# One batch's loads moved to another DMA queue and later in the order, with its features re-dealt between two engines

## The chip, the cores and the metric

The kernel runs on one core of a Trainium2 chip. The metric is the device time of one execution in microseconds (us). The core has a matrix engine (TensorE, PE in the profile; its weight loads are listed as PEld), a vector engine (VectorE, DVE), a scalar engine (ScalarE, ACT), GpSimd (POOL) and SyncE (SP). SP does no arithmetic here: it only issues DMAs. A name with a q behind it (SPq, POOLq) is the instruction queue of that engine.

## The reference

Eight batches of cosine-weighted linear attention (8 heads, 576 positions, 64 dimensions) feed a two-layer network with a squared ReLU between its layers.

```python
def phi(x, c, s):
    r = np.maximum(x, 0.0)
    return np.concatenate([r * c, r * s], axis=-1)
q_p = phi(q, cos_w, sin_w)
k_p = phi(k, cos_w, sin_w)
kv = np.einsum('bhsf,bhsd->bhfd', k_p, v)
z = np.sum(k_p, axis=2)
num = np.einsum('bhsf,bhfd->bhsd', q_p, kv)
den = np.einsum('bhsf,bhf->bhs', q_p, z)[..., None] + 1e-06
x = (num / den)          # to [batch * position, head * dimension] = 4608 x 512
h = x @ w_in             # 512 -> 2048
g = np.maximum(h, 0.0) ** 2
out = g @ w_out          # 2048 -> 512
```

All inputs and the output are float32; the products run in bf16.

## The kernel before

**Attention of one batch.** The 576 positions are cut in four pieces of 128 (j = 0 to 3) and a tail of 64 (j = 4). For each batch b and piece j there are these steps, each a small function:

- `load_batch`, `load` (L61 to L77): three tensors from HBM, each as one DMA of 1 MB and two of 64 KB (the tails, `kt`, `vt`, `qt`). The input buffers are double, so batch 3 reuses batch 1's.
- `att_k` (L190): the features of k, a cosine half and a sine half, `kp`. The sine half is always made by ACT (`feat_sin`, L181), the cosine half by DVE (`feat_cos`, L171) or ACT (`feat_cos_act`, L186).
- `att_v` (L194): a copy of v to bf16, `vext`, by DVE or ACT (L200).
- `att_kv` (L222): the products of k features and v on PE (`kz`, L241), in two parts, and a copy of the sum to `kvz` by ACT.
- `att_feat` (L254): the features of q, `qp`, cosine half by DVE, sine half by ACT.
- `att_qT` (L259): from batch 2 on, the transposition of `qp` by a DMA that SP issues (L267), two pieces at a time: `qpT<-qp` twice, `qpT<-qpt` for the tail.
- `att_d`: `att_num` on PE (`num`, L310) and `att_div` on DVE (L320 to L324), which writes `x`.
- `att_x` (L331): from batch 2 on, the transposition of `x` by a DMA that SP issues (L342): `xT<-x` twice, `xTt<-xt` for the tail.

**The two layers of the network.** They are cut in slots of about 1.75 us of PE work. `gemm1` (L361) is the first layer: 16 or 32 matmuls into a PSUM tile `hps` (L383), then a ReLU on ACT (`rt`, L391) and a square on DVE (`gT`, L398). The first half of a batch's slots reads the first `xT`, the second half the second. `gemm2` is the second layer. From batch 1's second pair on it is a seven-product scheme (`pair_mm`, L541): products `p1` to `p7` go through four PSUM tiles `ya`, `yc`, `yu`, `yv`, each used for one product after another. A tile is free again only when ACT has copied it (`s1`, L561, `s5`, L576) or DVE has added it on (L537). `hps`, `yu` and `yv` share two PSUM buffers in turn.

**The order.** Everything is in the order of the program text. There are 144 slots, numbered from 0. A table `after` tells what is emitted behind each slot, and it is filled by calls `at(slot, function, ...)`, mostly through `plan` (L625). Work registered for the same slot is emitted in the order of registration. The slots that matter here:

| slots | work on PE | start in the profile, us |
|---|---|---|
| 16 to 25 | batch 1, layer 1 | 53.75 |
| 26 to 33 | batch 1, layer 2 | 74.82 |
| 34 to 41 | batch 2, layer 1 (34 to 37 read the first `xT` of batch 2, 38 to 41 the second) | 91.56 |
| 42 to 49 | batch 2, layer 2 (two pairs) | 109.81 |
| 50 to 59 | batch 3, layer 1 | 123.62 |

Batch 3's attention runs beside slots 27 to 41, batch 4's beside slots 42 to 54, and so on. `first[b]` and `second[b]` are the numbers of a batch's first slots of layers 1 and 2 (`second[2]` is 42, `first[3]` is 50).

**The queues.** Batch 0's inputs are loaded by SP. The weights and the inputs of batches 1, 2 and 3 are loaded by POOL, batch 3's behind slot 14. From batch 4 on SP loads, with k and v at one slot and q at a later one. SP's list is therefore, in this order: batch 2's three query transposes, then transposes of `x` of batch 2 and of queries of batch 3 in turn, with the k and v loads of batch 4 among them. The results of batches 0 to 6 are written by POOL (`put`, L401), one DMA of 512 KB for two pieces. Each SP DMA also waits, before it is issued, until the DMA eight places earlier in that list has landed; eight semaphores are used in turn.

Of the kernel before, what the change touches and what calls it, by code (L numbers as in the profile page):

```python
# [19 lines left out]
def kernel(  # L20
# [9 lines left out]
    nc = tc.nc  # L30
# [13 lines left out]
    NS = J + 1  # L44
# [562 lines left out]
    slots, first, second = [], {}, {}  # L607
# [6 lines left out]
    def at(s, fn, *args):  # L614
        after.setdefault(s, []).append((fn, args))
# [6 lines left out]
        att_qT_pe(b, j)  # L622
        att_qT_copy(b, j)

    def plan(b, k, f, kv, d, t=(), x=(), shared=True):  # L625


        for j in range(NS):
            last = j == J or j % 2
            at(k[j], att_k, b, j, feat_cos_act if shared and j % 2 else feat_cos)  # L630
            at(k[j], att_v, b, j, nc.scalar if shared and (b > 2 or j % 2) else nc.vector)
            at(f[j], att_feat, b, j)
            if t:
                at(t[j], att_t, b, j)
            elif last:
                at(f[j], att_qT, b, j // 2)
            at(d[j], att_d, b, j)
            if x:
                at(x[j], att_x_pe, b, j, x[j] > 16)
            elif last:  # L640
                at(d[j], att_x, b, j // 2)
        for i in range(2):
            at(kv[i], att_kv, b, i)


    for j in (2, 3):
# [8 lines left out]
    at(18, att_d, 0, J)  # L655
    at(19, att_x_pe, 0, J, True)
    plan(
        1,
        k=(8, 8, 8, 9, 9),
        f=(4, 5, 6, 12, 13),  # L660
        kv=(10, 10),
        d=(11, 13, 15, 17, 19),
        t=(5, 6, 7, 16, 17),
        x=(12, 14, 16, 18, 20),
        shared=False,
    )
    at(14, load_batch, 3, nc.gpsimd, "qkv")
    plan(
        2,
        k=(21, 22, 23, 24, 25),  # L670
        f=(18, 19, 20, 22, 23),
        kv=(26, 26),
        d=(27, 28, 29, 31, 33),
    )
    plan(
        3,
        k=(30, 32, 33, 34, 35),
        f=(27, 29, 31, 32, 33),
        kv=(36, 36),
        d=(37, 38, 39, 40, 41),  # L680
    )
    for b in range(4, B):
        o, p = second[b - 2], first[b - 1]
        at(second[b - 3] + 6, load_batch, b, nc.sync, "kv")
        at(first[b - 2] + 9, load_batch, b, nc.sync, "q")
        plan(
            b,
            k=(o, o, o + 1, o + 1, o + 2),
            f=(o + 4, o + 4, o + 5, o + 5, o + 6),
            kv=(o + 3, o + 4),  # L690
            d=[p + j for j in range(NS)],
        )

# [95 lines left out]
```

## Time and profile before

| what | value |
|---|---|
| median of 4 runs | 294.12 us (293.37 to 296.67) |
| the profiled execution | 294.11 us |
| its span, first to last instruction | 292.2 us |
| PE busy | 281.7 us, 96% of the span |
| DVE, ACT, POOL busy | 201.7, 164.7, 39.0 us |
| moved by DMA | 53.04 MB, mean 181 GB/s |
| matrix clock granted | 1.00 |

In the profile a group of instructions is shown as `line engine op out<-in`. A timeline line gives the start in us from the start of the span, the duration in us, and the count (x16). Brackets at its end give the time that the engine stood idle just before, and what ended that idle time. A DMA issue is timed by its issuing instruction; the DMA view adds the time from issue to landing.

### The profile page before, as it was taken

The page shows a single profiled execution, that of the slowest core. Times are in us where ns is not written, and L with a number is a line of the kernel's source. Part 1 is how long each engine was busy: PE and PEld are TensorE (multiplying, and loading weights), DVE is VectorE, ACT ScalarE, POOL GpSimd, SP SyncE. Part 2 cuts the span into 40 slices and gives each one's busy share as a digit, 9 for nine tenths or more (in the row PEclk, how much of TensorE's full clock was granted, in tenths as well). Part 3 has the DMA queues.
Part 4 walks back from the last instruction along what each step waited for, and adds up shares of the span by engine and source line. Part 5 has one row for each costly group of instructions (what it writes and reads, how often), then busy time and mean ns, then how long its engine had stood idle before and what let it go on. Part 6 is the DMA issues. An engine that isn't in the chain of part 4 may idle for free.

```text
span 292.2 us, 7292 instructions
## 1 busy us (share of the span) xinstructions
PE 281.7 (96%) x3045; PEld 236.4 (81%) x3045; DVE 201.7 (69%) x450; ACT 164.7 (56%) x251; POOL 39.0 (13%) x67
## 2 busy tenths in 40 slices
PE   8999999998999979999999999999999999999994
PEld 3469855788668969898988888988998988889883
DVE  2367765596399497977688777977677877546584
ACT  3476653679748758645783258835595551165110
POOL 1462504850000000000002000000000000000011
PEclk9999999999999999999999999999999999999999
DMA  7999995999638996699619995299718520300014
GB/s 208 291 203 285 343 219 174 341 375 295 101 103 159 283 199 194 163 266 284 190 71 189 291 236 164 82 249 305 184 56 206 141 46 2 143 3 2 0 76 142
DMA packets 76641, 53.04 MB, mean 181 GB/s; under 512 B 52000, under 2 KB 71712, under 8 KB 76608
## 3 DMA queue, kind: packets, MB, share of 16 engines
q1 hardware_dynamic: 66816, 29.24, 43.2%
q0 software_dynamic: 9648, 23.20, 26.8%
q8 instruction: 24, 0.39, 0.5%
q10 hardware_dynamic: 144, 0.13, 0.1%
q14 instruction: 9, 0.07, 0.1%
HBM read 36.70 MB, written 9.44 MB: 158 GB/s over the span
## 4 chain that ended last, share of the span: by engine, by line
PE 75%; DMA 10%; DVE 5%; ACT 3%; issue 2%; SPq 2%; POOL 1%; DVEq 0%; POOLq 0%
PE hps L383 36%; PE ya L525 9%; PE yc L525 8%; PE yu L525 7%; DMA q<-in_q_dram 6%; PE yv L525 4%; PE num L310 3%; PE kz L241 3%; DMA out_dram<-ysb 2%; PE yps L456 2%; DMA qpT<-qpt 2%; DVE ysb L537 1%; ACT rt L391 1%; SPq L69 1%; PE yps L432 1%
## 5 line engine op out<-in xcount | busy, mean ns | idle before, releaser
L383 PEld LDWEIGHTS <-w1sb 128*128 128x128 bf16 x1312 | 112.9, 98 | 13.7 <-issue 2.9
L383 PE MATMUL hps<-xT,w1sb 128*128 128x256 bf16 (+1 forms) x1056 | 119.0, 269 | 1.1 <-DVE ysb L537 0.6
L391 ACT ACTIVATE rt<-hps 128x1024 bf16<-128x1024 f32 x72 | 73.7, 1024 | 66.7 <-PE hps L383 43.3
L398 DVE TENSOR_TENSOR gT<-rt 128x1024 bf16<-128x1024 bf16 x64 | 44.0, 687 | 21.3 <-ACT rt L391 21.3
L525 PEld LDWEIGHTS <-gs 128*128 128x128 bf16 x480 | 46.9, 98 | 5.5
L525 PEld LDWEIGHTS <-gT 128*128 128x128 bf16 x312 | 29.8, 98 | 3.5
L410 POOL DMA_DIRECT2D out_dram<-ysb x14 | 7.6, 543 | 173.7 <-DVE ysb L537 145.8
L181 ACT ACTIVATE kp<-k,sin_col 128x512 bf16<-128x512 f32 x32 | 22.4, 719 | 2.9 <-DMA k<-in_k_dram 2.9
L324 DVE TENSOR_TENSOR x<-num,rden 128x512 bf16<-128x512 f32 x32 | 22.1, 691 | 1.1
L181 ACT ACTIVATE qp<-q,sin_col 128x512 bf16<-128x512 f32 x32 | 22.1, 724 | 0.8 <-DMA q<-in_q_dram 0.8
L320 DVE TENSOR_SCALAR den<-num 128x8 f32<-128x8 f32 (+1 forms) x40 | 6.5, 164 | 21.4 <-PE num L310 21.4
L521 DVE TENSOR_TENSOR gs<-gT 128x1024 bf16<-128x1024 bf16 x26 | 17.8, 685 | 0.0
L171 DVE TENSOR_SCALAR qp<-q,cos_col 128x512 bf16<-128x512 f32 x32 | 14.9, 492 | 1.8 <-DMA q<-in_q_dram 1.8
L383 PE MATMUL hps<-xTt,w1sb 128*128 128x128 bf16 x256 | 15.1, 219 | 0.8 <-ACT rt L391 0.8
L525 PE MATMUL yc<-w2sb,gs 128*128 128x256 bf16 x120 | 15.6, 273 | 0.0
L525 PE MATMUL ya<-w2t,gs 128*128 128x256 bf16 x120 | 15.6, 273 | 0.0
L525 PE MATMUL yu<-w2sb,gs 128*128 128x256 bf16 x120 | 15.6, 273 | 0.0
L525 PE MATMUL yu<-w2t,gs 128*128 128x256 bf16 x120 | 15.5, 272 | 0.0
L200 ACT CAST vext<-v 128x512 bf16<-128x512 f32 x23 | 14.2, 617 | 2.1 <-DMA v<-in_v_dram 2.1
L576 ACT COPY s<-yu 128x256 f32<-128x256 f32 x15 | 5.6, 373 | 17.3 <-PE yu L525 17.3
L310 PEld LDWEIGHTS <-qpT 128*128 128x128 bf16 (+1 forms) x240 | 10.3, 100 | 4.0 <-DMA qpT<-qpt 1.8
L525 PE MATMUL yc<-w2sb,gT 128*128 128x256 bf16 x104 | 13.5, 273 | 0.0
(93 smaller groups left out, 337.3 us busy)
## 6 DMA issues: line engine op xcount, KB each, us to landing
out_dram<-ysb POOLq DMA_DIRECT2D x14, 512.0 KB, 4.3
k<-in_k_dram SPq DMA_DIRECT2D x5, 1024.0 KB, 8.3
v<-in_v_dram SPq DMA_DIRECT2D x5, 1024.0 KB, 9.3
q<-in_q_dram SPq DMA_DIRECT2D x5, 1024.0 KB, 5.4
q<-in_q_dram POOLq DMA_DIRECT2D x3, 1024.0 KB, 12.6
k<-in_k_dram POOLq DMA_DIRECT2D x3, 1024.0 KB, 9.5
v<-in_v_dram POOLq DMA_DIRECT2D x3, 1024.0 KB, 8.5
w1sb<-in_moe_w_in_dram POOLq DMA_DIRECT2D x4, 512.0 KB, 9.1
```

The source lines that it names most:

```text
L171: nc.vector.tensor_scalar(out=dst[:, :, 0:D], in0=src, scalar1=0.0, scalar2=cos_col[:, j : j + 1], op0=ALU.max, op1=ALU.mult,)
L181: nc.scalar.activation(out=dst[:, :, D:F], in_=src, func=ACTF.Relu, scale=sin_col[:, j : j + 1])
L200: copy(out=vx[:, j, h0:h1, 0:D], in_=piece("v", b, j)[:, h0:h1, :])
L241: nc.tensor.matmul(out=kz[:, half, hh * E1 : (hh + 1) * E1], lhsT=lhsT, rhs=rhs, start=(j == 0 and hh == 0), stop=(j == J and hh == HH - 1),)
L310: nc.tensor.matmul(out=out, lhsT=lhsT, rhs=kvz[:, half * HH + hh, :], start=True, stop=True)
L324: nc.vector.tensor_tensor(out=x_of(b, j).rearrange("p (b k) (l d) -> p b k l d", b=n, l=2), in0=n4[:, :, :, 0:D].rearrange("p b (k l) d -> ...
L383: nc.tensor.matmul(out=out, lhsT=w1sb[:, kb, hb * P : (hb + 1) * P], rhs=rhs, start=(kb == 0), stop=(kb == KB - 1),)
L391: nc.scalar.activation(out=rt[:, :, :], in_=hps[:, :, :], func=ACTF.Relu)
L398: nc.vector.tensor_tensor(out=dst, in0=rt[:, :, :], in1=rt[:, :, :], op=ALU.mult)
L410: eng.dma_start(out=dst, in_=y.rearrange("p i c -> p (i c)") if n > 1 else y[:, c0:c1])
L521: nc.vector.tensor_tensor(out=t[:, :, :], in0=in0, in1=in1, op=op)
L525: nc.tensor.matmul(out=acc, lhsT=lhs[:, hb, :], rhs=rhs[:, hb, :], start=(hb == 0), stop=(hb == HB2 - 1),)
```

## The change

Four things are changed in `plan` and in the calls of `at`:

1. `load_batch(3, ...)` is moved from POOL at slot 14 (order q, k, v) to SP at slot 23 (order k, v, q). There it stands behind batch 2's third query transpose.
2. For batch 2, the cosine halves of k pieces 1 and 3 go from ACT to DVE, and so does the copy of v piece 3.
3. For batch 3, all cosine halves of k but the tail's go to ACT; the k and v slots are one or two earlier, the q feature slots three to six later, `att_kv` one later, and the divisions (`att_d`, with the transposes of `x` that follow them) two later, at slots 39 to 43.
4. For batch 4, the k and v loads go from slot 32 to slot 30. For batches 4 to 7, the two parts of `att_kv` go one slot later.

```diff
-    def plan(b, k, f, kv, d, t=(), x=(), shared=True):
+    def plan(b, k, f, kv, d, t=(), x=(), act_cos=(1, 3), act_v=range(NS)):
...
-            at(k[j], att_k, b, j, feat_cos_act if shared and j % 2 else feat_cos)
-            at(k[j], att_v, b, j, nc.scalar if shared and (b > 2 or j % 2) else nc.vector)
+            at(k[j], att_k, b, j, feat_cos_act if j in act_cos else feat_cos)
+            at(k[j], att_v, b, j, nc.scalar if j in act_v else nc.vector)
...
-        shared=False,
+        act_cos=(),
+        act_v=(),
     )
-    at(14, load_batch, 3, nc.gpsimd, "qkv")
     plan(
         2,
         k=(21, 22, 23, 24, 25),
         f=(18, 19, 20, 22, 23),
         kv=(26, 26),
         d=(27, 28, 29, 31, 33),
+        act_cos=(),
+        act_v=(1,),
     )
+    at(23, load_batch, 3, nc.sync, "kvq")
     plan(
         3,
-        k=(30, 32, 33, 34, 35),
-        f=(27, 29, 31, 32, 33),
-        kv=(36, 36),
-        d=(37, 38, 39, 40, 41),
+        k=(29, 30, 31, 32, 33),
+        f=(33, 34, 35, 36, 36),
+        kv=(37, 37),
+        d=(39, 40, 41, 42, 43),
+        act_cos=(0, 1, 2, 3),
     )
     for b in range(4, B):
         o, p = second[b - 2], first[b - 1]
-        at(second[b - 3] + 6, load_batch, b, nc.sync, "kv")
+        at(30 if b == 4 else second[b - 3] + 6, load_batch, b, nc.sync, "kv")
         at(first[b - 2] + 9, load_batch, b, nc.sync, "q")
         plan(
             b,
             k=(o, o, o + 1, o + 1, o + 2),
             f=(o + 4, o + 4, o + 5, o + 5, o + 6),
-            kv=(o + 3, o + 4),
+            kv=(o + 4, o + 5),
             d=[p + j for j in range(NS)],
         )
```

In SP's list the order around the change becomes: three query transposes of batch 2; k, v, q of batch 3 (nine DMAs); the first `xT` of batch 2; k, v of batch 4 (six DMAs); the second `xT` and the `xTt` of batch 2; three query transposes of batch 3; two `xT` and the `xTt` of batch 3; q of batch 4.

## The prediction

> **What bounds the kernel now.** I read the page first, then PE's timeline for its idle time, then the DMA views and SP's timeline between 60 and 140 us.
>
> ```profile
> span 292.2 us, 7292 instructions
> PE 281.7 (96%) x3045; PEld 236.4 (81%) x3045; DVE 201.7 (69%) x450; ACT 164.7 (56%) x251; POOL 39.0 (13%) x67
> PE 75%; DMA 10%; DVE 5%; ACT 3%; issue 2%; SPq 2%; POOL 1%; DVEq 0%; POOLq 0%
> ```
>
> PE is the bound. Whatever the change gains must be PE's idle time, and its timeline shows where that lies in the changed stretch:
>
> ```profile
> 73.03 1.95 PE L383 MATMUL hps<-xTt,w1sb 128*128 128x128 bf16 x32 [0.84 <-ACT rt L391]
> 78.01 0.30 PE L241 MATMUL kz<-vextt,kpt 64*128 64x65 bf16 x8 [0.33 <-ACT kpt L181]
> 91.56 5.40 PE L383 MATMUL hps<-xT,w1sb 128*128 128x256 bf16 x48 [0.63 <-DVE ysb L537]
> 109.56 0.32 PE L310 MATMUL num<-kvz,qpT 128*64 128x65 bf16 x8 [1.52 <-DMA qpT<-qpt]
> ```
>
> Four waits, 0.84 + 0.33 + 0.63 + 1.52 = 3.3 us: the most that can be gained, 1.1% of the time. (About 1% is also what a measurement of this kernel can tell from no change.) From 110 us on PE hardly waits, so nothing later can be won back.
>
> ```profile
> 83.65 1.23 SPq L342 DMA_TRANSPOSE xT<-x  x1
> 94.34 1.71 SPq L64 DMA_DIRECT2D k<-in_k_dram  x1
> 110.78 1.48 SPq L342 DMA_TRANSPOSE xTt<-xt  x1
> 112.31 0.57 SPq L64 DMA_DIRECT2D q<-in_q_dram  x1
> 118.24 0.53 POOL L410 DMA_DIRECT2D out_dram<-ysb  x1 [24.57 <-DVE ysb L537]
> ```
>
> The first `xT` of batch 2 is issued at 83.65, before any load in SP's list. The DMA view, for windows around single issues, gives its time to landing (3.0 us at 83.65) and that of one issued at 133.90 behind batch 5's k and v (5.0 us):
>
> ```profile
> xT<-x SPq DMA_TRANSPOSE x1, 3.0
> xT<-x SPq DMA_TRANSPOSE x1, 5.0
> q<-in_q_dram SPq DMA_DIRECT2D x1, 1024.0 KB, 5.4
> qpT<-qp SPq DMA_TRANSPOSE x1, 9.2
> ```
>
> The reader is to see that a transpose lands after what stands before it in the list (it landed at 138.89, v's last tail at 138.07), and that the query transpose issued at 64.81 took 9.2 us while POOL's loads of batch 3 ran.
>
> **What the Trainium skill says.** "DMA: Bandwidth & Descriptors", section Queues, rings and completion order: on each DMA engine descriptors are consumed in ring order. The trace agrees: SP's DMAs land in their order of issue from 60 to 140 us. The same page, section Issuing engines are not separate DMA queues: DMAs of all issuers share the same 16 engines; the 9.2 us show it. "PSUM — Partial Sum Buffer", section Engine vs sequencer instructions: ScalarE and VectorE are strict FIFO, so a feature that waits for a load holds up the PSUM copies behind it. The trace agrees in that every ACT and DVE instruction starts in program order.
>
> **Part 1, slots 20 to 33: the gain.** ACT loses two cosine halves (0.61 us from start to start) and one copy of v (0.51), 1.73 us of the stretch from 69.6 to 77 in which it runs without a pause. DVE takes 0.40 + 0.40 + 0.34 = 1.1 us there, where it waits 1.58 and 1.23 us for ACT: free. `rt` of slot 23 then starts at 71.36 instead of 71.98, so slot 25 starts at 72.3 instead of 73.03, and the tail's k feature is done before PE asks. Gain 1.1 us by slot 27. DVE loses five or more features of batch 3 (0.39 each) before slot 34, so its 0.63 us should go as well. Slot 34 could start at 91.56 - 1.1 - 0.6 = 89.9.
>
> **Part 2, the loads in SP's list: the loss.** The third query transpose of batch 2 waits for ACT's tail feature (now 73.4) and lands about 77.3. Behind it come 3.54 MB. After a change from transposes to loads the first tensor landed 4.4, 5.3 and 5.1 us after the last transpose (batches 4, 5, 7); I take 5.0. The next tensors follow at 3.3 to 4.2 us (batches 0, 2, 4, 5, 7); I take 3.7. POOL's write of batch 1's first results, 0.5 MB at about 84, takes the engines 1.6 us: in the packets from 127 to 128 us the write moved 0.34 MB and SP's ring 0.015. So k lands at 82.3, v between 86 and 87.6, q at 77.3 + 5.0 + 3.7 + 3.7 + 1.6 = 91.3.
>
> ACT wants k at 83.5 (there) and v at 84.8: it waits 1 to 3 us, and `s1` behind it is copied at about 87 to 88 where `p6` wants its tile at 86.8. That stall of up to 1.5 us is not added, since the next is longer: the first `xT` of batch 2, ready to issue at 82.4, stands behind these loads and lands 0.9 after q (as for batch 5), at 92.2. **Slot 34 starts at 92.2, not at 89.9.** Then k and v of batch 4 (4.2 + 3.7) and POOL's next write (1.6) stand before the second `xT`: 92.2 + 9.5 + 0.9 = 102.6. PE wants it after four slots and batch 3's `kz`, 4 x 1.75 + 1.36 = 8.4, at 100.6. **Slot 38 starts at 102.6.** Slot 42 follows after 4 x 1.75 and three `num` (0.24 each), at 110.3. Before it was 109.81, with two `num` more behind it: 109.3 at equal work. Loss +1.0 us, with all four old waits already credited. Bounds: loads at 326 GB/s throughout (batch 0's second and third tensor) give slot 34 at 90.4, slot 38 at 99.7, slot 42 at 107.4, -1.9 us; all costs at their upper ends give +3.
>
> The query transposes of batch 3 come next at 2.2 us each (512 KB): 105.3, 107.5, 108.3. `num` asks at 106.1 at the earliest, so the old 1.52 us wait does go.
>
> **Part 3, q of batch 4.** Its load stays at slot 43 but stands behind `xTt` of batch 3, which waits for the fifth division. That moves from slot 41 to 43. Counted from slot 42's start: `x` done at 4.8, `xTt` issued until 6.3 (1.48), q at +5.4 = 11.7. Before: issued 2.5, landed 7.9 to 8.4, used at 8.4: no slack. Now POOL's write of batch 2's first results (issued at 8.6) falls into it: +1.5, so 13.2. The users stay at slot 46. DVE stands at `qp` before the addition that frees `yc`: 13.2 + 0.8 + 0.35 = 14.4, where `p7` wants it at 12.3. Stall 2.1, of which 0.1 is made good at slot 50. Then `qpT` of batch 4 is issued at 14.5 and lands 4.2 later at 18.7, where `num` wants it at 18.0: 0.65. Together +2.6 us; without the clash with the write 1.1.
>
> **Parts at nothing.** `att_kv` one slot later for batches 4 to 7: `kvz` is used three or more slots later; if that cover were gone it would cost one 0.5 us copy each. Batch 5's k and v about 3.5 us later: landed at 138.07, used after 142.7 plus the delay. POOL's queue without nine DMAs lets batch 0's results leave earlier; nobody waits for them. The later divisions of batch 3 are used at slot 50: free.
>
> Sum: 294.11 + 1.0 + 2.6 = **297.7 us**. The profiled execution is at the median of 294.12, so no shift.
>
> **Rivals.**
> A, forecast: both `xT` and q late, 297.7, own range 296.0 to 299.5; chance 0.50.
> B, fast loads: -1.9 + 2.6 gives 294.8. For it: batch 0's second and third tensor. Against: after transposes the first tensor needed 5 us three times. Chance 0.22.
> C, slow loads: every cost of part 2 at its upper end (+3) and q's clash with the write at 2.1 instead of 1.5 us (+3.2) gives 300.3. For it: three writes of 0.5 MB fall into the stretch, and batch 5's k took 6.2 us from its first packet under one. Against: it needs all of them at once. Chance 0.20.
> D, not slower: the transposes do not stand behind the loads. Place: the first `xT` at slot 34. If it lands before 89.9 and the second before 98, all 3.3 us are gained, and q's delay of 1.1 to 2.6 is paid: 292.7. It decides from that landing. For it: batch 5's transpose lost only 2 us behind loads, because it was issued late. Against: no SP DMA overtook another. Chance 0.08. That the features' move brings nothing (ACT was not what held slot 25) would change the sum only by hiding 1.7 us of gain behind waits that end later anyway.
>
> **How the numbers follow.** Three quarters of A and all of C lie above 297.05 (+1%): 0.57 slower. The rest of A, B and most of D: 0.40 same. Faster by 1% needs all 3.3 us without q's price: 0.03. The range leaves out D, the low end of B and the high end of C: 294.5 to 300.5.
>
> **What would show it.** Right: PE waits at slot 34 for `xT` (about 2 us), at slot 38 (2 us), at `yc` near slot 48 (2 us), and no wait at slot 25, nor for `qpt` at slot 41. ACT waits for v. The first `xT` takes more than 6 us to land. Wrong: `xT` landing within 3 to 4 us of its issue, or q of batch 3 before 88.

## The result and the profile after

Over the timed executions (44 of the changed kernel, 63 of the kernel before) the ratio is **1.0072, 95% interval 1.0056 to 1.0088**: slower by 0.7%, which is 2.1 us on the 293.52 us that the kernel before had in this set. Ratios, here and below, leave out executions more than 1.5% above the fastest of their kernel (here 6 of the 44 and 2 of the 63), while medians, here 296.31 and 293.52 us or 0.95% apart, count all of them. The profiled execution took 297.63 us, 3.5 us more than the profiled one of before (294.11). The changed kernel's executions scatter more than those of before, 293.68 to 300.35 us, and the profiled one lies in the slower half. Times and profile are therefore kept apart below.

The page after, in its three lines on the whole:

```profile
span 295.9 us, 7290 instructions
PE 283.1 (96%) x3045; PEld 236.4 (80%) x3045; DVE 202.1 (68%) x451; ACT 164.2 (56%) x250; POOL 32.6 (11%) x58
PE 71%; DMA 16%; DVE 6%; POOL 2%; issue 1%; ACT 1%; SPq 1%; DVEq 0%; ACTq 0%
```

DMA's share of the chain that ended last rose from 10% to 16%, but this tells little of the change: 33 of its 48 us are three loads before 41 us (`v` 8.6, `q` 14.1, `w2sb` 10.4), which the change does not touch. PE's timeline shows where the changed kernel waits (start, duration, what, and in brackets the idle time before it and what ended it):

```profile
72.53 1.95 PE L383 MATMUL hps<-xTt,w1sb 128*128 128x128 bf16 x32 [0.23 <-ACT rt L391]
92.69 8.83 PE L383 MATMUL hps<-xT,w1sb 128*128 128x256 bf16 x64 [2.65 <-DMA xT<-x]
102.65 3.67 PE L383 MATMUL hps<-xT,w1sb 128*128 128x256 bf16 x32
110.63 1.03 PE L525 MATMUL ya<-w2sb,gT 128*128 128x256 bf16 x8
124.98 1.03 PE L525 MATMUL yc<-w2sb,gs 128*128 128x256 bf16 x8 [1.39 <-DVE ysb L537]
127.09 1.91 PE L383 MATMUL hps<-xT,w1sb 128*128 128x256 bf16 x16 [0.20 <-DVE ysb L537]
```

The reader is to see three things. The wait of 0.84 us at slot 25 has shrunk to 0.23, and the waits at `kz`'s tail (0.33) and for `qpt` (1.52) are gone. Slot 34, at 92.69, now waits 2.65 us for the first `xT` of batch 2. And near 125 us PE waits 1.39 us for an addition on DVE. DVE came late to that addition because it had stood waiting for q of batch 4, and so had ACT, as their timelines show:

```profile
123.71 0.88 DVE L171 TENSOR_SCALAR qp<-q,cos_col 128x512 bf16<-128x512 f32 x2 [2.15 <-DMA q<-in_q_dram]
124.51 0.42 DVE L537 TENSOR_TENSOR ysb<-yc,s 128x256 f32<-128x256 f32 x1
123.71 1.33 ACT L181 ACTIVATE qp<-q,sin_col 128x512 bf16<-128x512 f32 x2 [4.47 <-DMA q<-in_q_dram]
```

The DMA view for windows around the first `xT` and around q of batch 4 gives 8.5 us from issue to landing where before it was 3.0, and 6.3 where it was 5.4:

```profile
xT<-x SPq DMA_TRANSPOSE x1, 8.5
q<-in_q_dram SPq DMA_DIRECT2D x1, 1024.0 KB, 6.3
```

With q it is less the transfer than its issue that is late: 117.44 us instead of 112.31, since it stands behind `xTt` of batch 3, issued at 116.22 instead of 110.78.

One more thing shows in the line at 92.69: its 64 matmuls took 8.83 us, where four slots of 1.75 us make 7.0. The view by stretches has the granted clock (PEclk) in its third column from the right:

```profile
core 0: us, PE busy (x) PEld busy (x) DVE busy (x) ACT busy (x) POOL busy (x), PEclk, DMA share, GB/s
95.00:97.00 2.00, 2.00 (x12) 1.36 (x10) 0.45 (x1) 1.51 (x2) 0.00 (x0) 0.50 1.12 350
97.00:99.00 2.00, 2.00 (x20) 1.79 (x19) 0.64 (x2) 1.07 (x3) 0.00 (x0) 1.00 1.08 376
```

Behind the wait the matrix clock was at half from 93.6 to 97.0 us, 3.4 us in all, a loss of 1.7 us that PE shows as work and not as a wait.

Counted by stretches of the two profiled executions, slot 34 starts 1.1 us later than before (92.69, 91.56), slot 42 0.8 us later (110.63, 109.81, with two `num` of 0.24 us still to do), slot 50 3.5 us later (127.09, 123.62). From slot 50 to the end both need the same: 168.8 and 168.6 us.

### The profile page after: what moved, and what is told of

Read it like the earlier page. It is cut to its first block, busy times and chain, and to the rows that moved or that the text cites. A ratio compares the mean times of both kernels' runs of the same rounds, so it can differ in the third digit from the quotient of the medians.

```text
span 295.9 us, 7290 instructions
## 1 busy us (share of the span) xinstructions
PE 283.1 (96%) x3045; PEld 236.4 (80%) x3045; DVE 202.1 (68%) x451; ACT 164.2 (56%) x250; POOL 32.6 (11%) x58
## 4 chain that ended last, share of the span: by engine, by line
PE 71%; DMA 16%; DVE 6%; POOL 2%; issue 1%; ACT 1%; SPq 1%; DVEq 0%; ACTq 0%
PE hps L383 36%; PE ya L525 7%; DMA q<-in_q_dram 7%; PE yc L525 7%; PE yu L525 6%; PE yv L525 4%; DMA w2sb<-in_moe_w_out_dram 4%; DMA v<-in_v_dram 3%; DMA xT<-x 3%; PE num L310 2%; PE kz L241 2%; PE yps L456 2%; PE yh L432 2%; PE yps L432 2%; DVE ysb L537 1%
## 5 line engine op out<-in xcount | busy, mean ns | idle before, releaser
L383 PE MATMUL hps<-xT,w1sb 128*128 128x256 bf16 (+1 forms) x1056 | 120.4, 272 | 3.2 <-DMA xT<-x 2.7
L200 ACT CAST vext<-v 128x512 bf16<-128x512 f32 x22 | 13.5, 614 | 2.2 <-DMA v<-in_v_dram 2.2
L525 PE MATMUL ya<-w2sb,gT 128*128 128x256 bf16 x104 | 13.5, 272 | 0.0
L525 PE MATMUL yv<-w2t,gT 128*128 128x256 bf16 x104 | 13.5, 273 | 0.0
```

Source lines behind the costliest of these rows:

```text
L200: copy(out=vx[:, j, h0:h1, 0:D], in_=piece("v", b, j)[:, h0:h1, :])
L383: nc.tensor.matmul(out=out, lhsT=w1sb[:, kb, hb * P : (hb + 1) * P], rhs=rhs, start=(kb == 0), stop=(kb == KB - 1),)
L525: nc.tensor.matmul(out=acc, lhsT=lhs[:, hb, :], rhs=rhs[:, hb, :], start=(hb == 0), stop=(hb == HB2 - 1),)
```

## The experiments

The queue theory says that two transfers that became late make the loss: the first `xT` of batch 2 behind batch 3's loads (and the second behind batch 4's), and q of batch 4 behind `xTt` of batch 3. The rivals: the halved clock is a cost of its own; the re-dealt features cost by themselves; the order of the loads does not matter, only what POOL writes. The first two experiments take away one late transfer each, the next three look at the loads' order and at the clock, then come the combination of the first two, the features, and another split of the loads.

**q of batch 4 early** (label e1_q4_early).

```diff
-        at(first[b - 2] + 9, load_batch, b, nc.sync, "q")
+        at(38 if b == 4 else first[b - 2] + 9, load_batch, b, nc.sync, "q")
```

> The changed kernel with one load moved: q of batch 4 is issued at slot 38, behind batch 3's query transposes, instead of slot 43 behind its xTt. Queue theory (the loss is made of two late transfers, the first xT of batch 2 and q of batch 4): ACT's 4.5 us and DVE's 2.2 us wait for q near 123 us vanish, PE's 1.39 us at yc and 0.20 us at slot 50 with them, and the time falls by 1.6 to 2.2 us against the changed kernel, to about the kernel before (ratio 0.998 to 1.002). The wait of about 2.6 us for the first xT stays. Rival (the re-dealt features are what costs, or a wait behind q takes its place): the time falls by less than 0.5 us.

Measured: ratio 1.0023 (0.9996 to 1.0050), median 294.97 us. Against 1.0072 the time falls by 0.5%, 1.4 us. PE's and ACT's timelines, near the place where the changed kernel stood for q:

```profile
120.05 1.33 ACT L181 ACTIVATE qp<-q,sin_col 128x512 bf16<-128x512 f32 x2
124.34 1.04 PE L525 MATMUL yc<-w2sb,gs 128*128 128x256 bf16 x8
```

No brackets: neither ACT nor PE waits there any more. The wait for the first `xT` stays at 2.65 us as expected. A wait that was not expected stands at slot 38:

```profile
103.58 3.67 PE L383 MATMUL hps<-xT,w1sb 128*128 128x256 bf16 x32 [1.31 <-DMA xT<-x]
```

The second `xT` took 8.8 us from issue to landing instead of 6.9. It stands before the moved load in SP's list, so the move did not push it back; what did was not found. (The profiled execution, 296.76 us, is slower than this kernel's median, so its span is not compared.) The 1.4 us are a little less than the 1.6 to 2.2 expected and more than the rival's 0.5: q's lateness is real, and in the timed executions it is cheaper than in the profile.

**Batch 3's loads back on POOL** (e2_b3_on_pool).

```diff
+    at(14, load_batch, 3, nc.gpsimd, "qkv")
...
-    at(23, load_batch, 3, nc.sync, "kvq")
```

> The changed kernel with batch 3's loads back on POOL at slot 14, in the order q, k, v; everything else as changed. Queue theory: the first xT of batch 2 lands about 3 us after its issue, slot 34 starts at about 89.9 us without a wait, the halved matrix clock after the wait (3.4 us at half speed, 1.7 us lost) does not come, and all four old waits of the kernel before (0.84, 0.33, 0.63, 1.52 us) stay gone or nearly so; q of batch 4 is still late (1.6 to 2.6 us). Time about 1 us below the kernel before (ratio 0.994 to 0.999), 3 us below the changed kernel's profile. Rival 1 (the re-dealt features cost by themselves): still above the kernel before by 0.5% or more. Rival 2 (the query transposes of batch 2 are again late behind POOL's loads, and the gain at slots 25 to 27 is lost there): ratio 0.998 to 1.003 with a wait at the first num of batch 2.

Measured: ratio 0.9987 (0.9961 to 1.0014), median 293.11 us, 0.85% or 2.5 us below the changed kernel. PE at slot 34, the first `xT` in the DMA view, and PE at `yc`:

```profile
89.59 1.59 PE L383 MATMUL hps<-xT,w1sb 128*128 128x256 bf16 x13
xT<-x SPq DMA_TRANSPOSE x1, 3.3
120.26 1.03 PE L525 MATMUL yc<-w2sb,gs 128*128 128x256 bf16 x8 [1.30 <-DVE ysb L537]
```

Slot 34 starts at 89.59 us without a wait (89.9 was worked out), the clock stays full there, and q's wait remains. So it was the place of batch 3's loads and not the features that made slot 34 late: with the features as changed, the kernel before is reached again. Rival 1 falls. The gain of about 1 us on the kernel before is not shown: 0.1% is at the edge of what was expected, and the interval includes 1. This run puts the loads back in queue and in time at once. That their place in SP's list matters is shown by the next run, where the same transpose lands 3.6 us after its issue with q behind it; loads issued by POOL as late as slot 23 were not run.

**q of batch 3 behind the first xT** (e3_q3_behind_xT).

```diff
-    at(23, load_batch, 3, nc.sync, "kvq")
+    at(23, load_batch, 3, nc.sync, "kv")
+    at(28, load_batch, 3, nc.sync, "q")
```

> The changed kernel with batch 3's q taken out of the block: k and v at slot 23 as changed, q at slot 28 behind the first xT of batch 2. Queue theory: the first xT lands near 87 us and the wait at slot 34 (2.65 us) goes, but the second xT of batch 2 stands behind as many bytes as before and lands near 102 us as in the changed kernel; PE, which is now early, waits 2 to 3 us for it at slot 38. The time falls by 0 to 1 us only against the changed kernel. Rival (only the first xT matters): slot 38 starts near 99 us and the time falls by 3 us or more.

Measured: ratio 1.0172 (1.0130 to 1.0214), median 298.96 us: slower than the changed kernel by 1.0%, where 0 to 1 us less was expected. PE's timeline and the clock of a stretch behind the second wait:

```profile
94.02 3.65 PE L383 MATMUL hps<-xT,w1sb 128*128 128x256 bf16 x32 [0.88 <-ACT rt L391]
102.49 1.89 PE L383 MATMUL hps<-xT,w1sb 128*128 128x256 bf16 x8 [3.61 <-DMA xT<-x]
104.00:106.00 2.00, 2.00 (x11) 1.44 (x10) 0.00 (x0) 0.00 (x0) 0.00 (x0) 0.50 1.21 270
```

The mechanism came as stated: the wait at slot 34 is gone and reappears at slot 38, 3.61 us for the second `xT`, which could not start earlier than in the changed kernel (102.49, 102.65). What was missed is the price behind it: the clock was at half for 6.8 us (100.8 to 107.6, from the middle of the wait on), which by the trace cost slots 38 to 41 about 2.6 us. Also ACT stood 0.82 us for q of batch 3, and PE 0.88 us for the `rt` behind it: an engine in fixed order passes a late load on.

**The wait filled with dummy matmuls** (e4_filled_wait).

```diff
+    at(33, fill_y, 11)
...
+    def fill_y(n):
+        wm = ps_y.tile([P, FP], F32, name="wm", tag="yps", bufs=2)
+        for i in range(n):
+            nc.tensor.matmul(
+                out=wm[:, :], lhsT=ident[:, :], rhs=zeros[:, :], start=True, stop=True
+            )
```

> The changed kernel with 11 dummy matmuls of 512 columns (about 0.22 us each) behind slot 33, which keep PE busy while it waits for the first xT of batch 2; their result is not used. Clock rival (the halved clock after the wait is a cost of its own): no stretch at half clock near 93 to 97 us, slots 34 to 37 take 7.0 us instead of 8.7, and the time falls by about 1.7 us. Queue theory: the clock stays full too, but the second xT then lands (about 102 us) after slot 38 could start (101 us), so a wait of about 1 us appears there and the time falls by 0.5 to 0.7 us only.

Measured: ratio 1.0084 (1.0060 to 1.0108), no faster than the changed kernel's 1.0072. PE's timeline and one of the stretches:

```profile
89.52 2.55 PE L226 MATMUL wm<-zeros,ident 128*128 128x512 bf16 x11
101.70 3.67 PE L391 MATMUL hps<-xT,w1sb 128*128 128x256 bf16 x32 [1.45 <-DMA xT<-x]
94.00:96.00 2.00, 2.00 (x21) 1.80 (x19) 1.09 (x2) 1.89 (x3) 0.00 (x0) 1.00 1.03 368
```

The clock stays at 1.00, and what it saves turns into a wait of 1.45 us at slot 38 for the second `xT`. So the halved clock was not an extra cost here: it lay beside the time that the second `xT` needed anyway. In this trace the clock rival falls for the change (not for the experiment before). The 0.5 us that were expected to be left did not show in the times. The times alone could not decide it, since the 11 matmuls (2.55 us) are added work in every execution in which the first `xT` comes early.

**Dummy matmuls, and batch 4's k and v back at slot 32** (e8_filled_kv4_late), from the kernel with the filled wait.

```diff
-        at(30 if b == 4 else second[b - 3] + 6, load_batch, b, nc.sync, "kv")
+        at(second[b - 3] + 6, load_batch, b, nc.sync, "kv")
```

> The changed kernel with the dummy matmuls of the filled wait behind slot 33 and, in addition, k and v of batch 4 back at slot 32, so that the second xT of batch 2 stands before them. Queue theory: the second xT lands near 94 us, the 1.45 us wait at slot 38 goes; batch 3's query transposes stand behind the same loads as before and land 0 to 1 us after num asks, so 0 to 1 us of it comes back there. Time 0.5 to 1.5 us below the changed kernel (ratio to the kernel before 1.002 to 1.006). Rival (the write by POOL and not the order sets when batch 2's second xT lands): the wait at slot 38 stays over 1 us.

Measured: ratio 1.0094 (1.0075 to 1.0112), from 5 executions, not the 1.002 to 1.006 expected. In the profile the places are as stated: no wait at slot 38, and instead

```profile
105.75 0.42 PE L318 MATMUL num<-kvz,qpT 128*128 128x65 bf16 x8 [0.79 <-DMA qpT<-qp]
```

a wait for batch 3's query transpose, now behind those loads. From slot 34 to slot 50 this profile needs 33.3 us, 0.9 less than the one before it, but its first 54 us were 0.8 us longer (slot 16 starts at 54.25 instead of 53.41), in code that neither experiment touches. The second `xT` now landed 5.0 us after its issue, before PE asked, although POOL wrote beside it (its write was issued at 91.65): the order sets which transfer is late, and the rival that only POOL's writes count falls. Whether this order is any faster is not settled by these runs.

**Both late transfers undone** (e5_pool_q4_early): batch 3 on POOL at slot 14 and q of batch 4 at slot 38, the first two diffs together.

> Both late transfers undone: batch 3's loads on POOL at slot 14, and q of batch 4 at slot 38 on SP; everything else as changed. Queue theory: the 1.3 + 0.2 us that PE still waited at yc and slot 50 with the loads on POOL go, no other wait over 0.3 us is left between 60 and 130 us, and the time is 2 to 3 us below the kernel before (ratio 0.990 to 0.995), below both kernels. Rival (q early is paid elsewhere, as waits for the transposes of x behind it): ratio 0.997 to 1.001.

Measured: **ratio 0.9939 (0.9919 to 0.9959), median 291.53 us: faster than both kernels**, as expected. The two gains add up: 0.49% and 0.85% singly, 1.33% together. On another chip it is again 0.9921 (0.9893 to 0.9949) (label e11_pool_q4_same_chip):

> The kernel with batch 3 on POOL and q of batch 4 at slot 38 once more, for the comparison on one chip with the split loads. Expected: 0.991 to 0.996, and 0 to 0.3% slower than the split loads.

PE's waits from 60 to 130 us in the first of its profiles, all of them:

```profile
72.42 1.95 PE L383 MATMUL hps<-xTt,w1sb 128*128 128x128 bf16 x32 [0.23 <-ACT rt L391]
81.05 0.42 PE L310 MATMUL num<-kvz,qpT 128*128 128x65 bf16 x8 [1.93 <-DMA qpT<-qp]
112.64 0.32 PE L310 MATMUL num<-kvz,qpT 128*64 128x65 bf16 x8 [0.16 <-DVE x L324]
```

`yc` and slot 50 no longer wait. In this execution, at 293.6 us the slowest of its nine, a new wait of 1.93 us stands at the first `num` of batch 2: the query transpose behind POOL's loads, the very thing that the change moves out of the way. In the profile of the kernel with the loads on POOL alone the same transposes were in time. The expectation of no wait over 0.3 us failed on it.

The profiled execution on the other chip took 297.00 us, more than either kernel's median, and its ratio does not count it. Its trace has the same wait, longer, and the view by stretches shows the engines while that transpose was under way:

```profile
82.64 0.42 PE L310 MATMUL num<-kvz,qpT 128*128 128x65 bf16 x8 [4.19 <-DMA qpT<-qp]
68.00:82.00 14.00, 10.11 (x134) 7.66 (x134) 5.78 (x14) 8.69 (x13) 0.00 (x0) 1.00 1.26 127
```

The transpose took 18.5 us to land, and behind the wait the clock was at half for 3.4 us. From 68 to 82 us, with this transpose, the last of batch 3's loads and two writes by POOL on them, the DMA engines moved only 127 GB/s, though their share of busy time did not fall (1.26); from 64 to 66 us it was 330 GB/s at a share of 1.04. Why they are so slow together is not shown. So the kernel with both transfers undone is the faster one, but 1 of its 17 executions on record is slower than the median of either kernel, by the very wait that moving the loads off POOL avoids.

**Batch 2's features as before in that kernel** (e9_pool_q4_b2_as_before).

```diff
-        act_cos=(),
-        act_v=(1,),
+        act_cos=(1, 3),
+        act_v=(1, 3),
```

> As the kernel with batch 3 on POOL and q of batch 4 at slot 38, but with batch 2's features dealt as in the kernel before (cosine halves of k pieces 1 and 3 and v pieces 1 and 3 on ACT). Claim of part 1: 1.1 us (0.4%) slower than that kernel, with the waits of about 0.8 us at slot 25 and 0.3 us at the tail of kz back. Rival (with the loads on POOL the wait moves to batch 2's query transposes in both): no difference.

Measured beside the kernel with both transfers undone, on the same chip: 0.9975 (0.9962 to 0.9988) against 0.9939, medians 292.49 and 291.53 us. The two old waits are back:

```profile
72.49 1.95 PE L383 MATMUL hps<-xTt,w1sb 128*128 128x128 bf16 x32 [0.84 <-ACT rt L391]
77.46 0.30 PE L241 MATMUL kz<-vextt,kpt 64*128 64x65 bf16 x8 [0.33 <-ACT kpt L181]
```

In this kernel the re-dealing is worth about 1 us (0.36%), as part 1 had it.

**Batch 2's features alone, in the kernel before** (e7_before_b2_dealt).

```diff
+            on_act = shared and (b > 2 or j % 2) if v_act is None else j in v_act
+            at(k[j], att_v, b, j, nc.scalar if on_act else nc.vector)
...
         d=(27, 28, 29, 31, 33),
+        shared=False,
+        v_act=(1,),
```

> The kernel before with one part of the change alone: batch 2's cosine halves of k all on DVE, and of its v copies only piece 1 on ACT. Claim of the prediction's part 1: the waits of 0.84 us at slot 25 and 0.33 us at the tail of kz shrink to 0.2 and 0, slot 27 is reached 1.1 us earlier; nothing behind it is bound to a fixed time, so the time falls by about 1 us (ratio 0.995 to 0.998). Rival (the gain is absorbed by the waits at slots 34 and 41, which end by DMA and DVE): the waits of 0.63 and 1.52 us grow by 1 us together and the ratio is 0.999 to 1.001.

Measured: ratio 1.0001 (0.9985 to 1.0017). In the profile the gain is there and nothing absorbs it: 0.23 us at slot 25, none at `kz`'s tail, and the two later waits no longer than before (0.63 and 1.34 us).

```profile
90.16 5.40 PE L383 MATMUL hps<-xT,w1sb 128*128 128x256 bf16 x48 [0.63 <-DVE ysb L537]
107.98 0.32 PE L310 MATMUL num<-kvz,qpT 128*64 128x65 bf16 x8 [1.34 <-DMA qpT<-qpt]
```

Inconclusive: the times speak for the rival, since their interval leaves out the 0.995 to 0.998 expected; the profile speaks for the claim, since the rival's longer waits are not in it. What takes the microsecond back in the timed executions was not found.

**Loads split between the queues** (e10_q3_sp_kv3_pool), from the kernel with both transfers undone.

```diff
-    at(14, load_batch, 3, nc.gpsimd, "qkv")
+    at(14, load_batch, 3, nc.gpsimd, "kv")
...
+    at(23, load_batch, 3, nc.sync, "q")
```

> As the kernel with batch 3 on POOL and q of batch 4 at slot 38, but batch 3's loads split: k and v on POOL at slot 14, q on SP at slot 23 behind batch 2's query transposes. In the profile of that kernel the query transposes, behind 3.5 MB of POOL's loads, were 1.93 us late for the first num of batch 2 in the profiled execution. Queue theory: with 2.4 MB in front the first query transpose lands near 72 us instead of 76, the second near 76, no wait at num; q lands near 80 us and the first xT, issued at 82 to 84, is not delayed. Ratio to the kernel before 0.989 to 0.993, and a narrower spread of its runs. Rival (q on SP delays the first xT again): a wait at slot 34 of 0.5 us or more and a ratio above 0.995.

Measured: ratio 0.9916 (0.9884 to 0.9947), median 290.93 us, beside 0.9921 for the unsplit loads on the same chip: the lowest median of all, but no difference that these runs can tell. In its profile the query transposes are in time and slot 34 waits for nothing, yet the second `xT` was 1.88 us late:

```profile
100.32 3.67 PE L383 MATMUL hps<-xT,w1sb 128*128 128x256 bf16 x32 [1.88 <-DMA xT<-x]
```

That profiled execution took 293.38 us, the slowest of seven; the others lie between 290.42 and 291.42.

## Why the prediction was right, point by point

The forecast was 297.7 us, slower by 1.2%; the timed ratio says 0.7%. The direction and the mechanism (transposes and q of batch 4 late behind loads and divisions) were right and the size was 1.5 us too large. That the profiled execution came to 297.63, within 0.1 us, is luck: terms too large and too small cancelled, and most of the timed executions were faster.

- **What bounds the kernel, and the ceiling of 3.3 us.** Right. The four old waits were 3.3 us; in the changed kernel 0.23 us of them is left. With the late transfers undone the timed gain is 0.6% to 0.8%, 1.8 to 2.3 us.
- **Part 1, the features.** Right in place and nearly in size: slot 25 without 0.6 of its 0.84 us, slot 27 at 77.34 instead of 78.24. In the times it is 1 us in one pair of kernels and nothing in the other, where batch 2's features alone were changed.
- **Part 2, the order of landing.** Right, its times in part by luck. By the trace k landed at 81.4 (82.3 worked out), q's last tail at 91.8 (91.3), the first `xT` at 92.64 (92.2), the second at 102.07 (102.6). Slot 34 started at 92.69 (92.2), slot 38 at 102.65 (102.6), slot 42 at 110.63 (110.3). The three loads alone were faster than worked out (all but q's last tail was there at 88.95, where the sum without the write gives 89.7), and the write cost more: that tail came 2.9 us later, where 1.6 was put down.
- **Part 2, the lower bound.** The sum does not come out. At 326 GB/s 3.54 MB take 10.9 us; with the 1.6 of the write and the 0.9 of the transpose slot 34 starts at 90.7 and not at 90.4, slot 38 at 100.4, slot 42 at 108.1: -1.2 us instead of -1.9. Rival B would then stand at 295.5 instead of 294.8.
- **Part 2, what PE does between the two.** Wrong, without harm to the sum: a wait of 2 us at slot 38 was forecast, and a half-speed clock, which the prediction does not have, stood in its place. The experiment with the filled wait shows that one replaces the other.
- **Part 2, ACT waiting 1 to 3 us for v.** Wrong: v landed at 84.83 and ACT took it at 84.94. Two steps failed. POOL's write, issued at 84.1, met q's last tail instead of v, and landed itself only after 7.7 us. And even without the write v was put at 86.0, 1.2 us too late.
- **Part 3, q of batch 4.** Right in its cause. In the profile the loss from slot 42 to 50 is 2.65 us, of which two `num` are 0.49: 2.2 us, where 2.0 was forecast up to slot 50. Its parts differ: the stall at `yc` was 1.39 instead of 2.1, since `p7` reached its tile 0.7 us later than worked out, and that delay is part of the 2.2. Behind it the wait for batch 4's `qpT` in slot 50 was 0.2 instead of 0.65. In the times, however, the term is 1.4 us: there it was too dear.
- **Parts at nothing.** Right: from slot 50 on, where batches 4 to 7 have their later `att_kv`, nothing changed (168.6 and 168.8 us).
- **The size as a whole.** In the timed kernels the loads' place costs 2.5 us and q's delay 1.4; undoing both leaves a gain of about 1.8 us. 2.5 + 1.4 - 1.8 = 2.1, as measured. The forecast took each term from one profiled execution, and the changed kernel's executions spread over 7 us. Their granted clocks, which are on record, divide them. In 18 of the 44 the mean clock was 0.991 to 0.994 and the median time 297.6 us; in the other 26 it was 0.997 to 1.000 and the median 294.7. One stretch of 3.4 us at half clock makes 0.994 of a full clock over 296 us, so the 18 look like the profiled execution (0.993), as if PE had a long wait in each, and the 26 as if the transfers had been less late; of 110 executions of the kernel before whose clock is on record, only 3 are so low. The forecast fits the 18 and is 3 us too large for the 26. That a wait lies behind the low clock of executions without a trace is likely but not shown, and so is what makes the transfers late in one execution and not in the next: left open.

## What to carry to other kernels

A DMA queue in fixed order is a schedule like an engine's: before a block of loads is put into it, list what stands behind and when that is wanted. Here 3.5 MB of loads were hidden in themselves, and the 256 KB transpose behind them was not. A step that is moved later takes everything ordered behind it along, so the load of a quite different batch became late. And a change of several parts should be taken apart even when it loses: with its first part taken back, and one load moved up that its third part had made late, the other three made the kernel 0.6% faster than before.

## What the runs showed of the hardware that was not expected

An idle PE can cost more than its idle time. In four of the traces the clock went to half around a wait of PE: after 2.65 us without work for 3.4 us, in two kernels; around a wait of 3.61 us for 6.8 us; after 4.19 us for 3.4 us again. After waits of 1.34, 1.45, 1.52, 1.88 and 1.93 us it stayed full, so in these traces every wait from 2.65 us on did it and none up to 1.93 us, and the longest wait did not bring the longest stretch. The Trainium skill, "TensorE: Matmul & The Clock Gate", section HAM oscillation, warns of idle gaps over about 3.4 us; here a gap of 2.65 us was enough. Such a loss stands in no list of waits: it shows in the granted clock of a stretch and in matmul groups that are longer than their like. Whether it costs time depends on what comes next: in the changed kernel the next late transfer would have held PE nearly as long.
